# One wide matmul for two of three partial products in the last stage, results folded afterwards, one operand sum on POOL

## The chip, the cores and the metric

The kernel runs on one core of a Trainium2 chip. The metric is the time of one execution on the device in microseconds, the median of several runs. TensorE (PE in the rows, PEld for its weight loads) multiplies, VectorE (DVE in the rows) and ScalarE (ACT) work on tiles in SBUF and PSUM, GpSimd (POOL) on tiles in SBUF, and SyncE (SP) issues most of the DMA transfers.

## The reference

Attention over chunks of 32 positions, then two feed-forward blocks on 3072 tokens of 512 features, all in float32:

```python
x = attention(q, k, v, mem_k, mem_v)          # 3072 x 512
h = x @ w_in;  x = (h * tanh(softplus(h))) @ w_out
xn = x / sqrt(mean(x * x) + 1e-6) * rms_g
g = xn @ w_gate;  val = xn @ w_val            # 512 x 1536 each
out = (silu(g) * val) @ w_out                 # 1536 x 512
```

The change lies in the last product, `(silu(g) * val) @ w_out`.

## The kernel before

Every large product is done with two devices. First, a float32 operand is split into a high part (a rounded copy, made by ScalarE) and a low part (the rest, a subtraction on VectorE), and a product is the sum of high by high, high by low and low by high. Secondly, the matrices are cut into 2 x 2 blocks and multiplied in Strassen-Winograd fashion: seven block products instead of eight, on operands that are sums of blocks, and the results are put together by additions.

The last stage works in 12 units, one for each of three pairs of token groups and four row ranges (`units`, L1215, and the loop at L1252). A unit makes 256 rows of the output. Its input h was written to DRAM by the stage before and is loaded as four blocks of 128 x 768 (`h_load`, L867): a unit with an even number into the buffers raw, raw, sm and s, one with an odd number into parts of one weight slot, w. From the blocks come seven operands, which this text calls T1 to T7 by the number of the product (`h_pieces`, L885, and `sum_one`, L586). T1, T2, T3 and T7 are split from a block or a first sum, T5, T6 and T4 from a chain of three differences that are written into the same block: a difference on VectorE (L888), the high part on ScalarE (L153), the low part on VectorE (L154), then the next difference. The operands of unit n + 1 are made while TensorE works on unit n, one piece after each product (`preparing`, L1217). There are eight T buffers.

A product (`mul` in `group3`, L906) runs over six blocks of 128 features with three matmuls each, at L912 to L914: the high part of T with the high and the low part of the weights, and the low part of T with the high part of the weights. T is the operand that is loaded, the weights stream, and all three add into the same 256 columns of a PSUM bank. The weights w lie in SBUF as (7, 2, 256) per feature block: seven block operands, each with its high and its low part side by side. The results are put together in `group`, L643: two copies to SBUF on ScalarE (L649, L657), additions that read PSUM on VectorE (L654, L665, L668, L670), one sum on POOL (L669), and a last copy on ScalarE (L921). Two stores per unit are issued two pieces later (`store_later`, L104).

A scheduler of the framework orders the instructions of every engine by a timeline of its own (L19); each engine then executes its queue in that order. It issues the seven products of a unit in the order 1, 5, 6, 2, 4, 7, 3 and the operands as T1, T5, T6, T2, T4, T7, T3.

Of the kernel before, what the change touches and what calls it, by code (L numbers as in the profile page):

```python
# [13 lines left out]
ALU = mybir.AluOpType  # L14
# [10 lines left out]
W_AT = {1: 0, 2: 1, 4: 2, 3: 3, 5: 4, 6: 5, 7: 6}  # L25
# [4 lines left out]
def tile_kernel(  # L30
# [15 lines left out]
    nc = tc.nc  # L46
# [57 lines left out]
    def store_later(dst, src):  # L104
        late.append((tick[0] + 2, dst, src))
# [12 lines left out]
    wtab, wslot = {}, {}  # L118
# [37 lines left out]
    jobs, raws, n_load, n_raw, start = [], [], [0], [10 ** 6], [True]  # L156
# [387 lines left out]
    def att_list(j):  # L544

        out = []
        t0 = TPP * j
        for s in range(TPP + 4):
            for op, lag in (("e", 4), ("d", 3), ("c", 2), ("b", 1), ("a", 0)):
                t = t0 + s - lag  # L550
                if t0 <= t < t0 + TPP:
                    if op == "a" and t % SPB == 0:
                        out.append([(att_a0, t)])
                    out.append([(att_ops[op], t), (att_ops[op + "1"], t)])
        return out
# [13 lines left out]
    def s_new():  # L569
        return late_pools["s"].tile([128, 2, N2], F32, tag="s", name="s")  # L570

    def v_new(i):
        return late_pools[("gr", "gl")[i % 2]].tile([128, 2, N2], F32, tag="v", name="v")

    def c_new():
        return late_pools["c"].tile([128, N2], F32, tag="c", name="c")
# [9 lines left out]
    def sum_one(j, p, src, new, dram, tab):  # L586
        cols = src.shape[2]
        size = src.shape[1] * cols
        t = new()
        if isinstance(t, tuple):  # L590
            split(src, *t)
            for l in range(2):
                store_later(dram[:, p - 1, l].bitcast(F32), t[l].bitcast(F32))
            return
        v = t.rearrange("p l a n -> p l (a n)")[:, :, 0:size]
        v = v.rearrange("p l (a n) -> p l a n", n=cols)
        split(src, v[:, 0], v[:, 1])
        if dram is not None:
            store_later(dram[:, p - 1].bitcast(F32), t.bitcast(F32))
        tab[j, p] = v  # L600
# [42 lines left out]
    def group(mul, banks, n_, c12, c21, c22, temps, five_first=False):  # L643

        X, Y, Z, V = banks
        x, y, z, vv = (b_[:, 0:n_] for b_ in banks)
        s1, u2, z5 = temps()
        mul(1, X, True)
        nc.scalar.copy(s1, x)  # L649
        yield  # L650
        for p in (5, 6) if five_first else (6, 5):
            if p == 6:
                mul(6, Y, True)
                nc.vector.tensor_tensor(u2, y, s1, op=ALU.add)  # L654
            else:
                mul(5, Z, True)
                nc.scalar.copy(z5, z)  # L657
            yield
        mul(4, V, True)
        yield  # L660
        mul(2, X, False)
        yield
        mul(7, Y, False)
        u3 = s1
        nc.vector.tensor_tensor(u3, y, s1, op=ALU.add)  # L665
        yield
        mul(3, Z, False)
        nc.vector.tensor_tensor(c12, z, u2, op=ALU.add)  # L668
        nc.gpsimd.tensor_tensor(c22, u3, z5, op=ALU.add)  # L669
        nc.vector.scalar_tensor_tensor(  # L670
            c21, vv, -1.0, u3, op0=ALU.mult, op1=ALU.add
        )
        yield
# [25 lines left out]
    def run(parts, between):  # L699
        while parts:  # L700
            for part in list(parts):
                if next(part, "end") == "end":
                    parts.remove(part)
                else:
                    between()
# [3 lines left out]
    def group_banks(of):  # L709
        g = n_group[0]  # L710
        n_group[0] += 1
        return [bk[(4 * g + of - 4 + i) % of] for i in range(4)]
# [21 lines left out]
    n_v = [0]  # L734
# [23 lines left out]
    class Feed:  # L758
# [34 lines left out]
        def next(self, s):  # L793
            self.load(s + 3)
            self.split(s + 3)
            self.load(s + 5)
            return self.out.pop(0)
# [87 lines left out]
    def h_pieces(n):  # L885
        b11, b21, b12, b22 = hraw.pop(n)
        one = lambda p, src: sum_one(n, p, src, t_new2, None, ttab_h)
        sub = lambda out, a, b: nc.vector.tensor_tensor(out, a, b, op=ALU.subtract)  # L888
        early = [lambda: one(1, b11), lambda: sub(b11, b12, b11), lambda: sub(b12, b22, b12)]

        def p5():
            one(5, b11)
            sub(b11, b22, b11)

        def p6():
            one(6, b11)
            sub(b11, b11, b21)

        return early, [p5, p6, lambda: one(2, b21), lambda: one(4, b11),
                       lambda: one(7, b12), lambda: one(3, b22)]  # L900

    def group3(n, j, r, between):
        o = s_new()
        o = [o[:, a, :] for a in range(2)]

        def mul(p, bank_, first):  # L906
            t = ttab_h[n, p]
            ps = bank_[:, 0:256]
            more = dict(skip_group_check=not first)
            for f in range(HG):  # L910
                w = wtab["o2", f][:, W_AT[p]]
                nc.tensor.matmul(ps, t[:, 0, f], w[:, 0], start=first and f == 0, stop=False, **more)  # L912
                nc.tensor.matmul(ps, t[:, 0, f], w[:, 1], start=False, stop=False, **more)  # L913
                nc.tensor.matmul(ps, t[:, 1, f], w[:, 0], start=False, stop=f == HG - 1, **more)  # L914

        banks = group_banks(8)
        c11 = banks[0][:, 0:256]
        c12, c21, c22 = o[1][:, 0:256], o[0][:, 256:512], o[1][:, 256:512]
        run([group(mul, banks, 256, c12, c21, c22, lambda: (c_new()[:, 0:256], c12, c22),
                   True)], between)  # L920
        nc.scalar.copy(o[0][:, 0:256], c11)  # L921
        for a in range(2):
            row = (2 * j + a) * N2 + 128 * r
            store_later(out[row:row + 128, :], o[a])
# [24 lines left out]
    HG = F2 // 2  # L949
# [12 lines left out]
    first = att_list(0)  # L962
# [82 lines left out]
    units = [(1, i) for i in range(NHEAD)]  # L1045
    units += [(b, i) for i in (3, 4, 7, 5, 6) for b in range(2)]
    at = {u: 4 * n + 4 for n, u in enumerate(units)}
    more = {}
# [6 lines left out]
    more = {}  # L1055
# [10 lines left out]
    more = {}  # L1066
# [60 lines left out]
    for s, (m, i) in enumerate(steps):  # L1127
        t = feed.next(s)
# [18 lines left out]
        if m == NB2 - 1 and i in (1, 3, 5, 6):  # L1147
            row_slots.clear()
            f, u = {1: (2, 5), 3: (3, 6), 5: (4, 3), 6: (5, 2)}[i]
# [65 lines left out]
    units = [(j, r) for j in jback for r in range(NSUB2)]  # L1215

    def preparing(n, between):  # L1217

        st = dict(n=0)

        def fn():
            between()
            st["n"] += 1
            if st["n"] == 1:
                st["early"], st["rest"] = h_pieces(n)
                for call in st["early"]:
                    call()
            elif st["rest"]:
                st["rest"].pop(0)()

        return fn
# [20 lines left out]
    for n, (j, r) in enumerate(units):  # L1252
        if 0 < n < len(units) - 1:
            h_load(n + 1, *units[n + 1])
        group3(n, j, r, preparing(n + 1, flush) if n + 1 < len(units) else flush)
# [32 lines left out]
```

## Time and profile before

| | us |
|---|---|
| median of three runs (1165.23 to 1170.05) | 1168.31 |
| span of the profiled execution | 1167.0 |
| TensorE busy over the span | 1142.3 (98%) |
| VectorE busy | 824.7 (71%) |
| ScalarE busy | 628.7 (54%) |
| POOL busy | 183.3 (16%) |
| first matmul of the last stage | 979.76 |
| start of the last addition on VectorE | 1162.77 |

The page gives the span, which is 1.3 us under the median of the runs. Shares over the span are means over stages with different limits. The last stage takes the last 187 us of the span, so the windows and timelines of that stage are what counts. A matmul's row lasts longer than the distance to the next one, because matmuls are pipelined; the distance of starts is what it costs.

### The profile page before, as it was taken

The numbers are of one execution on the slowest core, as the hardware profiler recorded it, in microseconds if no ns is written. First come the engines' busy times: TensorE is split into PE (matmuls) and PEld (weight loads), VectorE is DVE, ScalarE is ACT, GpSimd is POOL, SyncE is SP. The second block draws the span as 40 slices with busy tenths as digits, with TensorE's granted clock in tenths as the row PEclk, the third lists the DMA queues.
The fourth block names the chain that finished last, engine by engine and source line by source line (L and its number), as shares of the span: only waits on it lengthen the run. The fifth ranks groups of instructions, "written<-read, shape, count | busy, mean of one in ns | idle before, by whom it ended". The sixth has DMA issues, their size and how long they took to land.

```text
span 1167.0 us, 22953 instructions
## 1 busy us (share of the span) xinstructions
PE 1142.3 (98%) x9052; PEld 1007.0 (86%) x9052; DVE 824.7 (71%) x1254; ACT 628.7 (54%) x1008; POOL 183.3 (16%) x165
## 2 busy tenths in 40 slices
PE   6899999999999999999999999999999999999998
PEld 4789999999999888888878778888888888999998
DVE  3555798844746876766786765967896857888883
ACT  4566666543555887667775543544454433444441
POOL 3011222310132321010011121110211111000000
PEclk9799999999999999999999999999999999999999
DMA  9889699899488764594599398999899879655421
GB/s 197 171 228 224 183 303 258 230 307 290 151 300 295 257 217 161 172 378 152 199 362 408 126 345 325 349 410 355 316 361 371 316 276 332 191 148 146 145 90 37
DMA packets 213276, 294.20 MB, mean 252 GB/s; under 512 B 104240, under 2 KB 160560, under 8 KB 204336
## 3 DMA queue, kind: packets, MB, share of 16 engines
q1 hardware_dynamic: 210864, 284.34, 73.6%
q0 software_dynamic: 2304, 8.39, 2.3%
q8 instruction: 71, 1.16, 0.4%
q14 instruction: 37, 0.30, 0.1%
HBM read 181.80 MB, written 110.89 MB: 251 GB/s over the span
## 4 chain that ended last, share of the span: by engine, by line
PE 83%; DVE 7%; DMA 5%; ACT 3%; issue 2%; SPq 0%; POOL 0%; ACTq 0%; DVEq 0%
PE bk L639 14%; PE bk L640 13%; PE bk L641 13%; PE bk L914 4%; PE bk L913 4%; PE bk L912 4%; PE bk L755 4%; PE bk L756 4%; PE bk L754 4%; PE bkp L639 2%; PE bkp L641 2%; PE bkp L640 2%; PE bkp L506 1%; PE bkp L457 1%; PE bkp L755 1%
## 5 line engine op out<-in xcount | busy, mean ns | idle before, releaser
L639 PE MATMUL bk<-T,w 128*128 128x384 f32 (+1 forms) x860 | 315.2, 370 | 0.7 <-ACT c L657 0.7
L640 PE MATMUL bk<-T,w 128*128 128x384 f32 (+1 forms) x860 | 311.3, 362 | 0.0
L641 PE MATMUL bk<-T,w 128*128 128x384 f32 (+1 forms) x860 | 308.3, 362 | 0.0
L639 PEld LDWEIGHTS bk<-T,w 128*128 128x128 f32 x860 | 162.3, 189 | 19.9 <-ACT c L657 1.0
L640 PEld LDWEIGHTS bk<-T,w 128*128 128x128 f32 x860 | 162.2, 189 | 16.5 <-DVE T L154 0.3
L641 PEld LDWEIGHTS bk<-T,w 128*128 128x128 f32 x860 | 161.8, 188 | 15.7
L913 PE MATMUL bk<-w,T 128*128 128x256 f32 x396 | 111.9, 283 | 0.0
L914 PE MATMUL bk<-w,T 128*128 128x256 f32 x396 | 111.9, 283 | 0.0
L912 PE MATMUL bk<-w,T 128*128 128x256 f32 x396 | 111.9, 283 | 0.0
L755 PE MATMUL bk<-T,w 128*128 128x512 f32 x276 | 107.5, 390 | 0.2 <-DVE T L154 0.2
L756 PE MATMUL bk<-T,w 128*128 128x512 f32 x276 | 107.1, 389 | 0.0
L754 PE MATMUL bk<-T,w 128*128 128x512 f32 x276 | 105.8, 389 | 0.0
L669 POOL TENSOR_TENSOR v<-c,v 128x512 f32<-128x512 f32 x36 | 54.7, 1519 | 289.2 <-DVE c L665 238.8
L665 DVE TENSOR_TENSOR c<-bk,c 128x512 f32<-128x512 f32 (+2 forms) x72 | 43.0, 597 | 51.2 <-PE bk L641 38.6
L912 PEld LDWEIGHTS bk<-w,T 128*128 128x128 f32 x396 | 76.0, 192 | 0.1
L913 PEld LDWEIGHTS bk<-w,T 128*128 128x128 f32 x396 | 76.0, 192 | 0.1
L914 PEld LDWEIGHTS bk<-w,T 128*128 128x128 f32 x396 | 76.0, 192 | 0.0
L649 ACT COPY c<-bk 128x512 f32<-128x512 f32 (+2 forms) x72 | 37.1, 516 | 69.6 <-POOL v L669 24.7
L154 DVE TENSOR_TENSOR T<-s,T 128x1024 fp32r<-128x1024 f32 (+1 forms) x50 | 63.1, 1269 | 14.3 <-ACT T L153 14.2
L782 ACT ACTIVATE s<-s 128x1024 f32<-128x1024 f32 x44 | 46.4, 1060 | 29.7 <-DMA s<-g_scratch 29.5
L755 PEld LDWEIGHTS bk<-T,w 128*128 128x128 f32 x276 | 51.8, 188 | 11.3 <-DVE T L154 0.6
L754 PEld LDWEIGHTS bk<-T,w 128*128 128x128 f32 x276 | 51.8, 188 | 10.8
(228 smaller groups left out, 2287.1 us busy)
## 6 DMA issues: line engine op xcount, KB each, us to landing
T<-nt_scratch SPq DMA_DIRECT2D x35, 1024.0 KB
g_scratch<-g SPq DMA_DIRECT2D x64, 384.0 KB
s<-g_scratch SPq DMA_DIRECT2D x46, 512.0 KB
h_scratch<-s SPq DMA_DIRECT2D x36, 512.0 KB
w<-wg SPq DMA_DIRECT2D x10, 1792.0 KB
wg<-w SPq DMA_DIRECT2D x30, 512.0 KB
raw<-in_moe_w_out_dram SPq DMA_DIRECT2D x28, 512.0 KB
nt_scratch<-T SPq DMA_DIRECT2D x14, 1024.0 KB
```

The costliest lines, as they stand in the source:

```text
L154: keep((eng or nc.vector).tensor_tensor(lo, src, hi.bitcast(F32), op=ALU.subtract))
L639: nc.tensor.matmul(ps, whi, xh, start=first and kk == 0, stop=False, **more)
L640: nc.tensor.matmul(ps, whi, xl, start=False, stop=False, **more)
L641: nc.tensor.matmul(ps, wlo, xh, start=False, stop=kk == 1, **more)
L669: nc.gpsimd.tensor_tensor(c22, u3, z5, op=ALU.add)
L754: nc.tensor.matmul(ps, ahi, bhi, start=start, stop=False)
L755: nc.tensor.matmul(ps, ahi, blo, start=False, stop=False)
L756: nc.tensor.matmul(ps, alo, bhi, start=False, stop=stop)
L782: nc.scalar.activation(x, g, self.act)
L912: nc.tensor.matmul(ps, t[:, 0, f], w[:, 0], start=first and f == 0, stop=False, **more)
L913: nc.tensor.matmul(ps, t[:, 0, f], w[:, 1], start=False, stop=False, **more)
L914: nc.tensor.matmul(ps, t[:, 1, f], w[:, 0], start=False, stop=f == HG - 1, **more)
```

## The change

In `group3` one matmul takes the high part of T with both halves of the weights, 512 columns, so that high by high lies in columns 0 to 255 of a bank and high by low in 256 to 511. A second matmul of 256 columns adds low by high to the upper half. All results stay 512 columns wide through the additions, and at the end a fold adds the upper to the lower half: four folds per unit on POOL (in the last unit on VectorE). The copy of product 5 goes to a tile of the pool `v`, the output's first block is copied at 512 columns to a tile of the pool `c`. In `h_pieces` the second difference of the early ones, b22 - b12, is made on POOL.

```diff
--- before.py
+++ after.py
@@ -885,8 +885,8 @@
     def h_pieces(n):
         b11, b21, b12, b22 = hraw.pop(n)
         one = lambda p, src: sum_one(n, p, src, t_new2, None, ttab_h)
-        sub = lambda out, a, b: nc.vector.tensor_tensor(out, a, b, op=ALU.subtract)
-        early = [lambda: one(1, b11), lambda: sub(b11, b12, b11), lambda: sub(b12, b22, b12)]
+        sub = lambda out, a, b, eng=nc.vector: eng.tensor_tensor(out, a, b, op=ALU.subtract)
+        early = [lambda: one(1, b11), lambda: sub(b11, b12, b11), lambda: sub(b12, b22, b12, nc.gpsimd)]
 
         def p5():
             one(5, b11)
@@ -902,23 +902,54 @@
     def group3(n, j, r, between):
         o = s_new()
         o = [o[:, a, :] for a in range(2)]
+        n_v[0] += 1
+        z5 = v_new(n_v[0])[:, 0, :]
+        end = n == len(units) - 1
 
         def mul(p, bank_, first):
             t = ttab_h[n, p]
-            ps = bank_[:, 0:256]
-            more = dict(skip_group_check=not first)
             for f in range(HG):
-                w = wtab["o2", f][:, W_AT[p]]
-                nc.tensor.matmul(ps, t[:, 0, f], w[:, 0], start=first and f == 0, stop=False, **more)
-                nc.tensor.matmul(ps, t[:, 0, f], w[:, 1], start=False, stop=False, **more)
-                nc.tensor.matmul(ps, t[:, 1, f], w[:, 0], start=False, stop=f == HG - 1, **more)
-
-        banks = group_banks(8)
-        c11 = banks[0][:, 0:256]
-        c12, c21, c22 = o[1][:, 0:256], o[0][:, 256:512], o[1][:, 256:512]
-        run([group(mul, banks, 256, c12, c21, c22, lambda: (c_new()[:, 0:256], c12, c22),
-                   True)], between)
-        nc.scalar.copy(o[0][:, 0:256], c11)
+                w = wtab["o2", f][:, W_AT[p]].rearrange("p l f -> p (l f)")
+                nc.tensor.matmul(bank_, t[:, 0, f], w, start=first and f == 0, stop=False,
+                                 skip_group_check=True)
+                nc.tensor.matmul(bank_[:, 256:512], t[:, 1, f], w[:, 0:256], start=False,
+                                 stop=f == HG - 1, skip_group_check=True)
+
+        def fold(out, x):
+            (nc.vector if end else nc.gpsimd).tensor_tensor(out, x[:, 0:256], x[:, 256:512], op=ALU.add)
+
+        def parts():
+            x, y, z, vv = group_banks(8)
+            s1 = c_new()
+            mul(1, x, True)
+            nc.scalar.copy(s1, x)
+            yield
+            mul(5, z, True)
+            nc.scalar.copy(z5, z)
+            yield
+            mul(6, y, True)
+            nc.vector.tensor_tensor(o[1], y, s1, op=ALU.add)
+            yield
+            mul(4, vv, True)
+            yield
+            mul(2, x, False)
+            c11 = c_new()
+            nc.scalar.copy(c11, x)
+            yield
+            mul(7, y, False)
+            nc.vector.tensor_tensor(s1, y, s1, op=ALU.add)
+            nc.vector.scalar_tensor_tensor(o[0], vv, -1.0, s1, op0=ALU.mult, op1=ALU.add)
+            nc.gpsimd.tensor_tensor(z5, s1, z5, op=ALU.add)
+            fold(o[0][:, 256:512], o[0])
+            fold(o[0][:, 0:256], c11)
+            yield
+            mul(3, z, False)
+            nc.vector.tensor_tensor(o[1], z, o[1], op=ALU.add)
+            fold(o[1][:, 0:256], o[1])
+            fold(o[1][:, 256:512], z5)
+            yield
+
+        run([parts()], between)
         for a in range(2):
             row = (2 * j + a) * N2 + 128 * r
             store_later(out[row:row + 128, :], o[a])
```

VectorE's queue while it makes the operands of an even unit (raw, sm, s), before; bk and bkp are PSUM banks, T an operand with its low part:

```order
L154 TENSOR_TENSOR T<-raw,T 128x768
L888 TENSOR_TENSOR raw<-sm,raw 128x768
L888 TENSOR_TENSOR sm<-s,sm 128x768
L654 TENSOR_TENSOR s<-bk_83,c 128x256
L154 TENSOR_TENSOR T<-raw,T 128x768
L888 TENSOR_TENSOR raw<-s,raw 128x768
L154 TENSOR_TENSOR T<-raw,T 128x768 x2
L888 TENSOR_TENSOR raw<-raw 128x768
L665 TENSOR_TENSOR c<-bk_83,c 128x256
L670 SCALAR_TENSOR_TENSOR s<-bk_85,c 128x256
L154 TENSOR_TENSOR T<-raw,T 128x768
L668 TENSOR_TENSOR s<-bk_84,s 128x256
```

The same stretch of VectorE's queue after:

```order
L154 TENSOR_TENSOR T<-raw,T 128x768
L888 TENSOR_TENSOR raw<-sm,raw 128x768
L154 TENSOR_TENSOR T<-raw,T 128x768
L888 TENSOR_TENSOR raw<-s,raw 128x768
L940 TENSOR_TENSOR c<-bk_83,c 128x512
L941 SCALAR_TENSOR_TENSOR s<-bk_85,c 128x512
L947 TENSOR_TENSOR s<-bk_84,s 128x512
L154 TENSOR_TENSOR T<-raw,T 128x768 x2
L888 TENSOR_TENSOR raw<-raw 128x768
L154 TENSOR_TENSOR T<-raw,T 128x768
L931 TENSOR_TENSOR s<-bk_87,c 128x512
L154 TENSOR_TENSOR T<-sm,T 128x768
```

The difference `sm<-s,sm` is gone from the queue, and the additions from PSUM (L931, L940, L941, L947) have 512 columns and stand elsewhere: L931 between the low parts of T4 and T7, where L654 stood in front of T5.

POOL's queue in the last stage, before (its end):

```order
L823 TENSOR_TENSOR w<-w 128x512
L824 TENSOR_TENSOR w<-w 128x512
L825 TENSOR_TENSOR w<-w 128x512
L669 TENSOR_TENSOR v<-c,v 128x512 x36
L669 TENSOR_TENSOR s<-c,s 128x256 x12
```

POOL's queue after, for an even and an odd unit from the middle of the stage (lines from L919 on are those of the kernel after):

```order
L888 TENSOR_TENSOR sm<-s,sm 128x768
L942 TENSOR_TENSOR v<-c,v 128x512
L919 TENSOR_TENSOR s<-s 128x256 x2
L919 TENSOR_TENSOR s<-c 128x256
L919 TENSOR_TENSOR s<-v 128x256
L888 TENSOR_TENSOR w<-w 128x768
L942 TENSOR_TENSOR v<-c,v 128x512
L919 TENSOR_TENSOR s<-s 128x256
L919 TENSOR_TENSOR s<-c 128x256
L919 TENSOR_TENSOR s<-s 128x256
L919 TENSOR_TENSOR s<-v 128x256
```

One instruction per unit became six: the difference (L888), the sum of product 5 (L942) and four folds (L919), the odd unit's in another order than the even one's.

## Rows read from the trace of the kernel before

**Rows 1.** VectorE and the others by window, the last stage

```profile
core 0: us, PE busy (x) PEld busy (x) DVE busy (x) ACT busy (x) POOL busy (x), PEclk, DMA share, GB/s
985.00:1160.00 175.00, 175.00 (x1461) 175.00 (x1460) 131.65 (x167) 72.49 (x112) 10.54 (x12) 1.00 0.46 136
```

**Rows 2.** Timeline of TensorE: start us, us, engine, line, tiles, shape, count

```profile
975.00 0.39 PE L641 MATMUL bkp<-T,w 128*128 128x512 f32 x1
...
976.36 0.39 PE L641 MATMUL bk<-T,w 128*128 128x512 f32 x1
...
979.54 0.39 PE L641 MATMUL bk<-T,w 128*128 128x512 f32 x1
979.76 0.28 PE L912 MATMUL bk<-w,T 128*128 128x256 f32 x1
...
1149.73 0.28 PE L913 MATMUL bk<-w,T 128*128 128x256 f32 x1
...
1151.89 0.28 PE L913 MATMUL bk<-w,T 128*128 128x256 f32 x1
```

**Rows 3.** Timeline of VectorE, operands of units 1 to 5, same columns

```profile
992.70 0.96 DVE L154 TENSOR_TENSOR T<-w,T 128x768 fp32r<-128x768 f32 x1 [4.40 <-ACT T L153]
...
1005.77 0.95 DVE L154 TENSOR_TENSOR T<-raw,T 128x768 fp32r<-128x768 f32 x1
1006.76 0.96 DVE L888 TENSOR_TENSOR raw<-sm,raw 128x768 f32<-128x768 f32 x1
1007.75 0.96 DVE L888 TENSOR_TENSOR sm<-s,sm 128x768 f32<-128x768 f32 x1
1008.67 0.96 DVE L154 TENSOR_TENSOR T<-raw,T 128x768 fp32r<-128x768 f32 x1
...
1018.28 0.95 DVE L154 TENSOR_TENSOR T<-w,T 128x768 fp32r<-128x768 f32 x1
...
1031.80 0.95 DVE L154 TENSOR_TENSOR T<-raw,T 128x768 fp32r<-128x768 f32 x1
...
1050.54 0.96 DVE L888 TENSOR_TENSOR w<-w 128x768 f32<-128x768 f32 x1
1052.45 1.83 DVE L154 TENSOR_TENSOR T<-w,T 128x768 fp32r<-128x768 f32 x2 [0.95 <-ACT T L153]
```

**Rows 4.** Waits, 980 to 1165 us: who waited for whom, us in total, times, longest

```profile
ACT T L153 <- DMA w<-h_scratch: 5.8, 1, 5.8
```

**Rows 5.** Instructions of line 912 by shape

```profile
L912 PE MATMUL bk<-w,T x396: 277/283/283, 979.8 to 1162.2; 128*128 128x256 f32 x198
...
L912 PE MATMUL bkp<-w,T x108: 283/283/283, 983.3 to 1147.1; 128*128 128x256 f32 x108
```

**Rows 6.** Timeline of VectorE, additions from PSUM, 512 and 256 columns

```profile
976.79 0.69 DVE L665 TENSOR_TENSOR c<-bk,c 128x512 f32<-128x512 f32 x1
977.40 0.68 DVE L654 TENSOR_TENSOR s<-bk,c 128x512 f32<-128x512 f32 x1
...
1041.58 0.42 DVE L670 SCALAR_TENSOR_TENSOR s<-bk,c 128x256 f32<-128x256 f32 x1
1041.91 0.41 DVE L668 TENSOR_TENSOR s<-bk,s 128x256 f32<-128x256 f32 x1
```

**Rows 7.** Instructions of line 669 on POOL: ns min/median/max, first and last start

```profile
L669 POOL TENSOR_TENSOR v<-c,v x36: 1286/1317/3272, 650.8 to 984.0; 128x512 f32<-128x512 f32 x36
...
L669 POOL TENSOR_TENSOR s<-c,s x12: 737/740/1336, 998.0 to 1161.2; 128x256 f32<-128x256 f32 x12
```

**Rows 8.** Timeline of VectorE beside a POOL sum

```profile
940.64 2.38 DVE L154 TENSOR_TENSOR w<-sm,w 128x512 fp32r<-128x512 f32 x2
...
1025.00 2.36 DVE L154 TENSOR_TENSOR T<-w,T 128x768 fp32r<-128x768 f32 x2
```

**Rows 9.** Timeline of POOL at the same places

```profile
940.02 1.84 POOL L669 TENSOR_TENSOR v<-c,v 128x512 f32<-128x512 f32 x1 [11.37 <-DVE c L665]
...
1025.30 1.24 POOL L669 TENSOR_TENSOR s<-c,s 128x256 f32<-128x256 f32 x1 [13.47 <-DVE c L665]
```

**Rows 10.** Timeline of VectorE, its last instruction

```profile
1162.77 0.42 DVE L668 TENSOR_TENSOR s<-bk,s 128x256 f32<-128x256 f32 x1 [1.22 <-PE bk L914]
```

## The prediction

> **What bounds the kernel now.** I read the busy shares by window first. Between 985 and 1160 us, the last stage, TensorE is busy all the time at full granted clock, VectorE 131.65 of 175 us, ScalarE 72 and POOL 10.5 [rows 1]. So TensorE sets the pace, and the next engine is VectorE. The timeline of TensorE gives the price of a matmul: 18 of 256 columns start in 2.16 us (1149.73 to 1151.89), 0.120 us each, and six of 512 columns in 1.36 us, 0.2267 us each, and the row of 256 columns behind one of 512 starts 0.22 us after it [rows 2]. Twice the columns costs 0.107 us more, which leaves 0.0133 us that every matmul pays whatever its width.
>
> The second question is how far VectorE is ahead, since it makes the operands T. The first one of unit 1 starts at 992.70, of units 2, 3 and 4 at 1005.77, 1018.28 and 1031.80 [rows 3]: 13.03 us per unit, while TensorE needs 42 x 0.360 = 15.12. VectorE gains 2.1 us on TensorE in each unit; that is all the room there is. It begins with almost none: unit 1's first cast waited 5.8 us for the h blocks to arrive [rows 4].
>
> **TensorE.** A product on one block of w was 3 x 0.120 = 0.360 us and is 0.2267 + 0.120 = 0.3467. There are 12 x 7 x 6 = 504 of them (396 + 108 rows of L912 [rows 5]): 504 x 0.0133 = 6.7 us less, and a unit is 42 x 0.3467 = 14.56 us. Whether the 13.3 ns belong to the matmul or to its change of weights makes no difference: one of each goes per product. The Trainium skill, "TensorE: Matmul & The Clock Gate", section "Back-to-back issue gap", gives a warm spacing of columns / 2.4 GHz plus about 2.5 ns; by it the saving would be an estimated 504 x 0.0025 = 1.3 us. The rows show 13.3 ns, and I go by them.
>
> **VectorE's own work.** Results are now 512 columns wide. In a row of such instructions each takes 0.61 us where one of 256 takes 0.33 (976.79 to 977.40, 1041.58 to 1041.91 [rows 6]). Four of 0.60 replace three of 0.33: +1.4 us per unit. The sum that goes to POOL gives back nothing: from the first difference to the low part of T5 it is 1.91 us with that sum in between (1006.76 to 1008.67) and 1.91 where none is in between (1050.54 to 1052.45) [rows 3], because ScalarE's cast lies there. ScalarE's wider copies fit into its idle half.
>
> I walk the queue of an even unit as the order after has it: independent instructions of 768 columns follow in 0.88 us (1.83 for two), dependent ones in 0.99, the difference to its low part is 1.91 [rows 3]. T1 0.00, first difference 0.99, T5 2.90, second difference 3.89, L940 4.76, L941 5.47, L947 6.07, T6 6.67, T2 7.54, third difference 8.41, T4 10.32, L931 11.19, T7 11.79, T3 12.66, next unit 13.53. The odd unit's order comes to 13.14. The same walk over the order of before gives 12.4 and 12.8, with 0.5 for its one POOL sum about 13.1, against 13.03 measured. So without POOL the units would be made in 13.3 us, under 14.56.
>
> **POOL.** This is the term that decides. Before, POOL does one sum of 256 columns per unit; after, one of 768, one of 512 and four of 256. Alone it takes 0.74 us for 256 and 1.29 to 1.32 for 512 [rows 7], so about 1.87 for 768 (estimate along that line), 6.1 us per unit. Where a POOL sum meets a VectorE instruction that reads two SBUF tiles, one stands still. At 1025.00 two low parts take 2.36 us instead of 1.83 while the sum of 256 beside them takes 1.24 instead of 0.74; at 940.64 two of 512 take 2.38 instead of 0.61 + 0.68, beside a sum of 512 with 1.84 [rows 3, 6, 8 and 9]. POOL waits for the running instruction, goes next, and VectorE then loses 0.53 us to 256 columns, 1.09 to 512, and by the same step 1.65 to 768: 4.9 us per unit if all of it lands on such instructions. Low parts and differences are of that kind; the four additions from PSUM are not, and while VectorE waits for a cast nothing is lost either.
>
> The walk again, with POOL in its order. The 768 sum can start when the first difference has ended (1.95, plus 0.2 until POOL moves) and holds to 3.8: T5 goes from 2.90 to 3.81. Second difference 4.80, L940 5.67, L941 6.38, L947 6.98. The sum of 512 runs from 6.5 to 7.6 under these three, so T6 loses 0.05 and starts at 7.63. The first two foldings are queued behind it; each gets in behind a VectorE instruction: T2 9.13, third difference 10.63 (0.63 late each, with POOL's start). The third folding fits into the wait for T4's cast, the fourth half: T4 12.86, L931 13.73, T7 14.33, T3 15.20, next unit 16.07. That is 2.5 us of the 4.9. In the odd unit L941 stands behind the second difference, and the last folding meets T7: 0.91 + 0.15 + 0.63 + 0.63 + 0.37 + 0.63 = 3.3, next unit 16.46. Mean 16.27 us, 1.7 over TensorE's 14.56. The bounds of this term are 0 (13.3 us) and 4.9 (18.2); I take 2.9, since the walk reproduces before.
>
> The Trainium skill, "SBUF — State Buffer", section "Who interferes with whom", has it that the loser blocks for the whole instruction of the other. By its full durations a fold would cost 0.74 instead of 0.53, an estimated 1 us more per unit than my walk. Rows 8 and 9 bear out the standstill, at the smaller price.
>
> **Sum.** VectorE now paces the stage. Unit 1's first operand still starts at 992.70, since it waits for a transfer that the change doesn't touch. Ten cycles later, at 992.7 + 162.7 = 1155.4, unit 11 starts; T4 is complete 13.6 later, at 1169.0, and TensorE, which takes the products in the order 1, 5, 6, 2, 4, 7, 3, has three left: 3 x 2.08 = 6.2. The last addition starts at 1175.3 where it was 1162.77 [rows 10]: +12.5. Behind it was one instruction of 0.42; now 0.71 for the wide addition to be done and two folds, 0.34 + 0.42: +1.05 to the output's transfers. Together +13.5 on the span of 1167.0; the page gives the span alone, and the runs' median is 1.3 over it. So 1168.3 + 13.5 = 1182.
>
> **Rivals.**
> *Operands keep ahead.* If the POOL sums fall into VectorE's waits for casts (2.0 us per unit) and under its four PSUM additions (2.4), all but 0.5 us is covered, a cycle is 13.8, TensorE stays the bound, and the time is 1168.3 - 6.7 + 1.05 = 1162.7. For it: of the walk's six meetings in an even unit, one costs nothing and one 0.05. Against it: foldings are issued back to back, and what is behind them are low parts. It decides the other way only if a cycle stays under 14.7. 20%, split evenly by the bound of half a per cent.
> *Half covered.* The end of the stage moves by 10.8 us per us of cycle (ten cycles and five sixths of one), so a cycle of 15.0 gives the time of before and 15.5 gives 1174. If foldings run later than I have them, into the next unit's first wait, 0.8 to 1.2 us of my 2.9 go: 1168 to 1174. 13%.
> *POOL in a heap.* If nothing is covered, 18.2 us per cycle, the time is about 1203. For it, POOL's own queue: late foldings delay the 768 sum, and T7 needs that. Against it, POOL has 10 us between the two. 5%.
> *The wide matmul brings nothing* (pitch 0.240): 1169 if TensorE were the bound. Rows 2 show 512 columns at 0.2267 in this kernel; 2%.
>
> **How the numbers follow.** The main case has 60%, with its own range of 1174 to 1191 (cycles of 15.5 to 17.1). Half a per cent, 5.8 us, is what a measurement here can tell from no change. Faster than 1162.5: half of the first rival, 0.10. Within: the other half, the half-covered case and the wide matmul's, 0.25. Slower: 0.65. The range goes from 1163 to 1191; it leaves out most of the first rival and the heap.
>
> **What would show it.** Right: in the last stage TensorE idles for some 1.5 us per unit, before the first matmul that needs a low part, released by VectorE; first low parts of units two apart are 32 to 33 us apart; low parts of 768 columns have a mean of 1.2 us or more instead of 1.0; POOL is busy for over 6 us per unit. TensorE's matmuls themselves start 0.227 and 0.120 apart. Wrong: TensorE busy without a gap and units at 14.6 us (the first rival), POOL's sums long but low parts at 0.95 (VectorE goes first, and POOL pays), or a first operand of unit 1 that comes well before 992, which would give VectorE a lead to live on.

## Result and the profile after

The changed kernel takes 1181.61 us (median of six runs, 1176.43 to 1185.49), the kernel before 1168.36 beside it (six runs, 1165.23 to 1170.05): a ratio of 1.0105, 95% interval 1.0088 to 1.0123. It is slower, at nearly the predicted time. The profiled execution took 1182.14 us with a span of 1180.4, 13.4 us over the span of before.

First the busy time by window in the last stage, in the columns of [rows 1]:

```profile
985.00:1175.00 190.00, 180.00 (x994) 151.28 (x992) 161.41 (x162) 78.58 (x114) 93.62 (x68) 1.00 0.44 129
```

TensorE, which had no gap before, is idle for some 10 us, at full granted clock. VectorE has gone from 75% to 85%, POOL from 10.54 us to 93.62. The waits of that stretch (engine, tile and line; what ended the wait; us in total, times, longest) say who is late:

```profile
PEld bk L915 <- DVE T L154: 11.0, 13, 1.7
PE bk L915 <- DVE T L154: 6.8, 13, 1.4
...
PEld bkp L915 <- DVE T L154: 4.2, 5, 1.0
PE bkp L915 <- DVE T L154: 2.6, 5, 0.7
```

These are TensorE's waits for a low part, 9.4 us on its matmuls (6.8 + 2.6). Between them the matmuls run at their pace, as TensorE's timeline shows behind the last wait:

```profile
1166.01 0.40 PE L913 MATMUL bk<-w,T 128*128 128x512 f32 x1
1166.25 0.28 PE L915 MATMUL bk<-w,T 128*128 128x256 f32 x1
...
1168.13 0.40 PE L913 MATMUL bk<-w,T 128*128 128x512 f32 x1
```

Six pairs in 2.12 us are 0.353 each; over all pairs without a stall the mean is 0.3494. Between 1075.70 and 1091.42 VectorE's queue makes an even unit, the walk of the prediction in real rows (start us, us, engine, line, operation, tiles, [idle before <- what ended it]):

```profile
1075.70 0.95 DVE L154 TENSOR_TENSOR T<-raw,T 128x768 fp32r<-128x768 f32 x1
1076.68 0.96 DVE L888 TENSOR_TENSOR raw<-sm,raw 128x768 f32<-128x768 f32 x1
1078.59 1.78 DVE L154 TENSOR_TENSOR T<-raw,T 128x768 fp32r<-128x768 f32 x1 [0.95 <-ACT T L153]
1080.41 0.96 DVE L888 TENSOR_TENSOR raw<-s,raw 128x768 f32<-128x768 f32 x1
1081.28 0.68 DVE L940 TENSOR_TENSOR c<-bk,c 128x512 f32<-128x512 f32 x1
1082.00 0.69 DVE L941 SCALAR_TENSOR_TENSOR s<-bk,c 128x512 f32<-128x512 f32 x1
1082.61 0.68 DVE L947 TENSOR_TENSOR s<-bk,s 128x512 f32<-128x512 f32 x1
1083.21 2.43 DVE L154 TENSOR_TENSOR T<-raw,T 128x768 fp32r<-128x768 f32 x2
1085.56 1.49 DVE L888 TENSOR_TENSOR raw<-raw 128x768 f32<-128x768 f32 x1
1088.01 1.16 DVE L154 TENSOR_TENSOR T<-raw,T 128x768 fp32r<-128x768 f32 x1 [0.96 <-ACT T L153]
1089.09 0.68 DVE L931 TENSOR_TENSOR s<-bk,c 128x512 f32<-128x512 f32 x1
...
1091.42 0.94 DVE L154 TENSOR_TENSOR T<-w,T 128x768 fp32r<-128x768 f32 x1
```

And POOL's in the same stretch, with its 768 sum (L888), its sum of 512 (L942) and the four folds (L919):

```profile
1077.72 1.84 POOL L888 TENSOR_TENSOR sm<-s,sm 128x768 f32<-128x768 f32 x1 [4.22 <-DVE raw L888]
1082.11 1.30 POOL L942 TENSOR_TENSOR v<-c,v 128x512 f32<-128x512 f32 x1 [2.55 <-DVE c L940]
1083.37 2.86 POOL L919 TENSOR_TENSOR s<-s 128x256 f32<-128x256 f32 x2
1086.19 1.45 POOL L919 TENSOR_TENSOR s<-c 128x256 f32<-128x256 f32 x1
1087.61 0.74 POOL L919 TENSOR_TENSOR s<-v 128x256 f32<-128x256 f32 x1
```

Lay one over the other. The low part of T5 is ready at 1078.59, but POOL holds on until 1079.56 and the 0.95 us become 1.78. The sum of 512 runs under additions from PSUM, and neither loses anything. The first three folds lie beside the low parts of T6 and T2 and the third difference: 2.43 instead of 1.83 and 1.49 instead of 0.95, while POOL needs 1.43 a fold instead of 0.74. The last fold lies mostly in a wait for a cast; T4's low part loses 0.21. That is 2.2 us in this unit. The odd one before it (from 1059.70) loses 2.9 by the same reading, 0.89 of it in the low part of T5 and the rest to the folds:

```profile
1062.55 1.84 DVE L154 TENSOR_TENSOR T<-w,T 128x768 fp32r<-128x768 f32 x1 [0.91 <-ACT T L153]
...
1066.82 2.42 DVE L154 TENSOR_TENSOR T<-w,T 128x768 fp32r<-128x768 f32 x2 [0.36 <-ACT T L153]
1069.16 1.49 DVE L888 TENSOR_TENSOR w<-w 128x768 f32<-128x768 f32 x1
...
1071.61 2.70 DVE L154 TENSOR_TENSOR T<-w,T 128x768 fp32r<-128x768 f32 x2 [0.36 <-ACT T L153]
```

### The profile page after: what moved, and what is told of

Read it like the earlier page. It is cut to its first block, busy times and chain, and to the rows that moved or that the text cites. A ratio compares the mean times of both kernels' runs of the same rounds, so it can differ in the third digit from the quotient of the medians.

```text
span 1180.4 us, 22026 instructions
## 1 busy us (share of the span) xinstructions
PE 1143.6 (97%) x8548; PEld 979.7 (83%) x8548; DVE 853.1 (72%) x1246; ACT 633.8 (54%) x1008; POOL 265.3 (22%) x221
## 4 chain that ended last, share of the span: by engine, by line
PE 66%; DVE 16%; DMA 7%; ACT 5%; issue 4%; SPq 1%; POOL 0%; ACTq 0%; DVEq 0%; POOLq 0%
PE bk L639 13%; PE bk L640 13%; PE bk L641 13%; DVE T L154 6%; PE bk L755 4%; PE bk L756 4%; PE bk L754 4%; ACT T L153 2%; DMA s<-g_scratch 2%; PE bkp L639 2%; PE bkp L640 2%; PE bkp L641 2%; DVE w L888 1%; PE bkp L506 1%; PE bkp L755 1%
## 5 line engine op out<-in xcount | busy, mean ns | idle before, releaser
L913 PE MATMUL bk<-w,T 128*128 128x512 f32 x396 | 138.8, 395 | 0.0
L915 PE MATMUL bk<-w,T 128*128 128x256 f32 x396 | 109.6, 284 | 6.8 <-DVE T L154 6.8
L913 PEld LDWEIGHTS bk<-w,T 128*128 128x128 f32 x396 | 73.5, 188 | 15.6
L915 PEld LDWEIGHTS bk<-w,T 128*128 128x128 f32 x396 | 74.6, 188 | 12.5 <-DVE T L154 11.0
L154 DVE TENSOR_TENSOR T<-s,T 128x1024 fp32r<-128x1024 f32 (+1 forms) x50 | 62.5, 1258 | 14.2 <-ACT T L153 14.2
L665 DVE TENSOR_TENSOR c<-bk,c 128x512 f32<-128x512 f32 (+1 forms) x60 | 38.0, 633 | 43.8 <-PE bk L641 41.6
L154 DVE TENSOR_TENSOR T<-w,T 128x768 fp32r<-128x768 f32 x42 | 53.5, 1295 | 15.2 <-ACT T L153 15.2
L153 ACT CAST T<-w 128x768 fp32r<-128x768 f32 x42 | 33.3, 832 | 55.5 <-DVE w L888 49.3
L649 ACT COPY c<-bk 128x512 f32<-128x512 f32 (+1 forms) x60 | 32.5, 543 | 56.4 <-POOL v L669 24.5
```

The costliest lines, as they stand in the source:

```text
L153: keep(nc.scalar.copy(hi, src))
L154: keep((eng or nc.vector).tensor_tensor(lo, src, hi.bitcast(F32), op=ALU.subtract))
L913: nc.tensor.matmul(bank_, t[:, 0, f], w, start=first and f == 0, stop=False, skip_group_check=True)
L915: nc.tensor.matmul(bank_[:, 256:512], t[:, 1, f], w[:, 0:256], start=False, stop=f == HG - 1, skip_group_check=True)
```

## The experiments

All times are medians, each with its ratio to runs of the kernel before on the same chip (1167.84 beside sum_back to no_folds, 1167.97 beside folds_write to narrow_last); the ratio is estimated from all runs and differs a little from the quotient of the two medians. "Stage" runs from the first to the last start of a matmul of the last stage; "cycle" is the distance of the first low parts (T1) of units 3 and 11 divided by eight; "low part" is the mean duration of L154 between 995 and 1155 us.

| kernel | median us | ratio [95%] | stage us | cycle us | low part ns |
|---|---|---|---|---|---|
| before | 1168.36 | 1 | 182.7 | 13.03 (units 1 to 4) | 996 |
| after | 1181.61 | 1.0105 [1.0088, 1.0123] | 193.5 | 15.86 | 1243 |
| sum_back | 1170.55 | 1.0021 [1.0003, 1.0039] | 183.0 | 15.01 | 1123 |
| folds_vector | 1169.78 | 1.0011 [0.9992, 1.0029] | 181.0 | 14.87 | 1023 |
| both_vector | 1164.11 | 0.9971 [0.9949, 0.9992] | 178.3 | 14.72 | 964 |
| no_folds | 1163.63 | 0.9969 [0.9946, 0.9992] | 179.3 | 14.49 | 977 |
| folds_write | 1164.12 | 0.9962 [0.9945, 0.9979] | 178.7 | 14.49 | 977 |
| folds_twice | 1179.79 | 1.0098 [1.0076, 1.0121] | 194.8 | 16.24 | 1237 |
| sum_only | 1167.88 | 0.9996 [0.9983, 1.0009] | 183.2 | 13.58 (units 1 to 4) | 1118 |
| narrow_last | 1165.35 | 0.9970 [0.9957, 0.9983] | 179.1 | 14.71 | 964 |

The theory, called the port theory in the expectations: VectorE's instructions on two SBUF tiles and POOL's sums exclude each other, and that is what makes the units longer. Two rivals: VectorE is late by its own work (wider additions, its order), and TensorE itself is the bound.

### sum_back: the 768 sum back on VectorE

```diff
-        early = [..., lambda: sub(b12, b22, b12, nc.gpsimd)]
+        early = [..., lambda: sub(b12, b22, b12)]
```

> The kernel after with b22 - b12 back on VectorE; folds stay on POOL. Port theory (a POOL sum stops VectorE's instructions that read two SBUF tiles): the sum of 768 no longer meets T5's low part (0.91 us per unit) and costs VectorE nothing itself, since it fills the wait for the cast: operand cycle 16.0 to about 15.1 us, time about 1172. Rival, VectorE's own queue (its wider additions and the order set the pace, POOL does not matter): 0.9 us per unit more on VectorE, about 1191. Rival, TensorE (the wide matmuls are slow): no change, 1182.

Measured: 1170.55, with a cycle of 15.01 instead of 15.86. VectorE has one more instruction of 768 columns in every unit and finishes each unit 0.85 us sooner. Low parts (L154, tiles of w) between 995 and 1155, by line and shape, after and then here (count | busy us, mean ns | idle before them, and its cause):

```profile
L154 DVE TENSOR_TENSOR T<-w,T 128x768 fp32r<-128x768 f32 x36 | 45.6, 1287 | 13.5 <-ACT T L153 13.5
```

```profile
L154 DVE TENSOR_TENSOR T<-w,T 128x768 fp32r<-128x768 f32 x39 | 44.5, 1162 | 8.4 <-ACT T L153 8.4
```

The mean falls by 125 ns. The rest of VectorE's queue has the same order in both kernels. Its own work cannot be what makes VectorE late.

### folds_vector and both_vector: the folds on VectorE

```diff
-            (nc.vector if end else nc.gpsimd).tensor_tensor(out, x[:, 0:256], x[:, 256:512], op=ALU.add)
+            nc.vector.tensor_tensor(out, x[:, 0:256], x[:, 256:512], op=ALU.add)
```

folds_vector keeps the 768 sum on POOL, both_vector has it on VectorE too.

> The kernel after with all folds on VectorE; the 768 sum stays on POOL. Port theory: four folds cost 1.9 us per unit as standstills (mean of the walk's 2.3 and 1.6) and 4 x 0.33 = 1.3 as VectorE's own work: cycle 16.0 to about 15.4, time about 1175. VectorE's own queue: 1.3 more, cycle 17.3, about 1196. TensorE: no change, 1182.

> The sum and the folds on VectorE; POOL keeps only the 512 sum of product 5. Port theory: 16.0 - 0.9 - 1.9 + 1.3 = 14.5, at TensorE's own pace: 1164 to 1169. VectorE's own queue: 16.0 + 0.9 + 1.3 = 18.2, about 1205. TensorE: 1182.

Measured: 1169.78 and 1164.11. The first came out better than expected: in its order L940, an addition from PSUM, lies in the first wait for a cast, beside the sum on POOL, and loses nothing to it; the low part of T5 behind it loses 0.37 us (1.32 instead of 0.95 at 1068.71) where it lost 0.83. The second, with the sum and the folds on VectorE, beats both kernels, by 0.3% over before. Its low parts, and its window from 995 to 1155:

```profile
L154 DVE TENSOR_TENSOR T<-w,T 128x768 fp32r<-128x768 f32 x40 | 37.9, 970 | 0.8 <-ACT T L153 0.8
```

```profile
995.00:1155.00 160.00, 159.74 (x911) 138.52 (x909) 150.34 (x205) 74.47 (x106) 19.55 (x12) 1.00 0.44 126
```

The same window of after:

```profile
995.00:1155.00 160.00, 150.79 (x831) 126.58 (x830) 141.09 (x141) 69.76 (x101) 82.50 (x60) 1.00 0.45 130
```

VectorE is busier (150.34 us against 141.09) and yet TensorE has next to no gap. Its timeline shows the four folds in 1.43 us (1068.18 to 1069.61), and that VectorE now waits for TensorE:

```profile
1068.18 0.75 DVE L919 TENSOR_TENSOR s<-s 128x256 f32<-128x256 f32 x2
1068.85 0.42 DVE L919 TENSOR_TENSOR s<-c 128x256 f32<-128x256 f32 x1
1069.19 0.42 DVE L919 TENSOR_TENSOR s<-v 128x256 f32<-128x256 f32 x1
...
1072.96 0.69 DVE L931 TENSOR_TENSOR s<-bk,c 128x512 f32<-128x512 f32 x1 [0.47 <-PE bk L915]
```

In after, the even unit shown above loses 1.35 us to the same folds on POOL (0.60 + 0.54 + 0.21), and the odd one 2.0 (0.59 + 0.54 + 0.87): VectorE saves nothing by giving them away, and on the mean of the two loses some 0.25 us.

### no_folds and folds_write: no folds, and POOL work that only writes

Both start from sum_back. no_folds leaves the four folds out; folds_write puts two fills in the place of each:

```diff
-            (nc.vector if end else nc.gpsimd).tensor_tensor(out, x[:, 0:256], x[:, 256:512], op=ALU.add)
+            for _ in range(2):
+                nc.gpsimd.memset(out, 0.0)
```

> Leaves the four folds of each unit out (the upper halves of the results are not added), sum on VectorE. Port theory: cycle 16.0 - 0.9 - 1.9 = 13.2, so TensorE is never short of operands and shows its own price: 0.347 us per pair of matmuls would give about 1162, the 0.351 to 0.353 that stretches of the trace after show about 1164. VectorE's own queue: 16.9, about 1191. TensorE: 1182.

> sum_back with each fold replaced by two POOL fills of the fold's output (256 columns each, so the upper halves are not added; POOL writes SBUF and reads none). Port theory (what collides is the reading of a second tile): VectorE runs as without folds, low parts of 768 columns at 0.99 us or less on average against 1.12 in sum_back, cycle under TensorE's 14.7, time like no_folds, about 1163. Rival (any POOL work on SBUF, or POOL's queue being full, slows VectorE): as sum_back, cycle 15.0, 1171.

Measured: 1163.63 and 1164.12, both with a cycle of 14.49, not 13.2: TensorE sets the pace. The 14.49 includes units in which the operands still gain on TensorE; from unit 5 to unit 11 it is 14.65, TensorE's 42 x 0.3494 = 14.67. In folds_write POOL fills (L920) while low parts run. Its timeline of POOL and VectorE, then its lines from 995 to 1155:

```profile
1071.15 2.08 POOL L920 MEMSET s<- 128x256 f32 x8
1071.16 1.82 DVE L154 TENSOR_TENSOR T<-raw,T 128x768 fp32r<-128x768 f32 x2
1072.89 0.95 DVE L888 TENSOR_TENSOR raw<-raw 128x768 f32<-128x768 f32 x1
```

```profile
L154 DVE TENSOR_TENSOR T<-w,T 128x768 fp32r<-128x768 f32 x41 | 38.9, 973 | 6.6 <-ACT T L153 6.6
...
L920 POOL MEMSET s<- 128x256 f32 x88 | 23.3, 310 | 19.9 <-DVE s L948 19.9
```

Two low parts in 1.82 and a difference in 0.95, the undisturbed times, with POOL at work until 1073.23. So it is not POOL's activity or its place in the program that stops VectorE. What a fold has and a fill has not is reads from SBUF; a fold alone also takes longer (0.74 us against 0.31), which these runs don't separate. The Trainium skill, "SBUF — State Buffer", section "Who interferes with whom", says that a VectorE instruction with two SBUF inputs contends with a POOL instruction that reads SBUF, and not with one that only writes; these rows agree.

### folds_twice: each fold on POOL twice

From sum_back; in two of the four folds a half is thereby added twice.

```diff
-            (nc.vector if end else nc.gpsimd).tensor_tensor(out, x[:, 0:256], x[:, 256:512], op=ALU.add)
+            for _ in range(1 if end else 2):
+                (nc.vector if end else nc.gpsimd).tensor_tensor(out, x[:, 0:256], x[:, 256:512], op=ALU.add)
```

> sum_back with every POOL fold executed twice, apart from the last unit's. Port theory: four more folds per unit at 0.53 to 0.63 us each, less what falls into waits for casts: cycle 15.0 to between 16.5 and 17.2, time about 1186 to 1194. Rival (VectorE's own queue sets the pace): no change, 1171.

Measured: 1179.79, in the right direction but under the expected range: +1.23 us per unit, 0.31 for an extra fold. The price of a meeting is unchanged (2.44 and 1.49 as in after), but not every extra fold makes a meeting of its own. POOL and VectorE in an odd unit:

```profile
1064.34 2.44 DVE L154 TENSOR_TENSOR T<-w,T 128x768 fp32r<-128x768 f32 x2 [0.35 <-ACT T L153]
1064.51 2.87 POOL L920 TENSOR_TENSOR s<-s 128x256 f32<-128x256 f32 x2
1066.70 1.49 DVE L888 TENSOR_TENSOR w<-w 128x768 f32<-128x768 f32 x1
1067.45 2.16 POOL L920 TENSOR_TENSOR s<-c 128x256 f32<-128x256 f32 x2
1068.12 0.68 DVE L948 TENSOR_TENSOR s<-bkp,s 128x512 f32<-128x512 f32 x1
1069.16 2.69 DVE L154 TENSOR_TENSOR T<-w,T 128x768 fp32r<-128x768 f32 x2 [0.36 <-ACT T L153]
```

The two folds from 1067.45 to 1069.61 lie for about half of their time under an addition from PSUM (0.68, undisturbed) and in a wait for a cast. The expectation had counted nearly every extra fold as a full meeting.

VectorE's queue has the same order in after, sum_back and folds_twice, but for the sum, so these three can be added up against each other. Over units 3 to 10 the low parts and differences take, beyond 0.95 us each, 2.54 us per unit in after, 1.70 in sum_back and 2.93 in folds_twice. The steps between them, -0.84 and +1.23, are those of the cycle (-0.85 and +1.23). In folds_write it is 0.06.

### sum_only: the kernel before with the 768 sum on POOL

```diff
-        early = [..., lambda: sub(b12, b22, b12)]
+        early = [..., lambda: sub(b12, b22, b12, nc.gpsimd)]
```

(`sub` takes the engine as in the change.)

> The kernel before with b22 - b12 on POOL and nothing else. As predicted (the sum costs VectorE nothing where it stood, and on POOL it holds up T5's low part by some 0.9 us): operands are made at 13.5 to 14 us per unit while VectorE catches up, instead of 13.03, TensorE (15.12 us per unit) stays the bound, time as before, 1168. Rival (the move relieves VectorE by a difference): 12.1 us per unit, the time as before too; the operand cycle of units 1 to 4 tells them apart.

Measured: 1167.88, the same as before. Its operands of units 1 to 4 are 13.58 us apart instead of 13.03 [rows 3], and the low part of T5 stands still beside the sum:

```profile
1006.54 0.96 DVE L888 TENSOR_TENSOR raw<-sm,raw 128x768 f32<-128x768 f32 x1
1007.58 1.85 POOL L888 TENSOR_TENSOR sm<-s,sm 128x768 f32<-128x768 f32 x1 [9.09 <-DVE raw L888]
1008.46 1.79 DVE L154 TENSOR_TENSOR T<-raw,T 128x768 fp32r<-128x768 f32 x1 [0.96 <-ACT T L153]
```

The same stall that is on the path in after costs nothing here, since TensorE needs 15.12 us a unit and the operands are ahead.

### narrow_last: both_vector with the last unit as before

```diff
-        run([parts()], between)
+        if end:
+            ...
+            run([group(mul1, banks, 256, c12, c21, c22, lambda: (c_new()[:, 0:256], c12, c22),
+                       True)], between)
+            nc.scalar.copy(o[0][:, 0:256], banks[0][:, 0:256])
+        else:
+            run([parts()], between)
```

(`mul1` is the old `mul`.)

> both_vector with the last unit in the form of before (narrow matmuls, no folds): from the last matmul's start to the end of the span 4.8 us instead of 6.3, while the last unit's matmuls take 42 x 0.0105 = 0.44 longer: about 1 us less than both_vector, 1163. If the folds behind the last matmul cost nothing, as both_vector, 1164.

Measured: 1165.35, 0.9970 of before; both_vector's 0.9971 has an interval that covers it. In the profile the tail is shorter: from the last matmul's start to the end of the span 4.1 us (1156.92 to 1161.0), where both_vector has 6.0 (1154.46 to 1160.5), while the stage is longer (179.1 instead of 178.3). The medians show nothing of the difference. Inconclusive.

## Why the prediction was right

*The pace.* Right: VectorE sets it, through POOL. The walk gave 16.27 us per unit; over units 1 to 11 it is 16.02 (994.71 to 1154.86), over units 3 to 11 15.86. The meetings cost 2.2 and 2.9 us where the walk had 2.5 and 3.3. They lie at the places it named, but that in the odd unit the sum of 512 cost nothing (the walk's second term there, 0.15); the rest of the difference is in the folds, each a little cheaper than the walk's (0.54 to 0.60 instead of 0.63, T4's 0.21 instead of 0.32, the odd unit's last pair 0.87 instead of 1.00). By the full block that the prediction cites, and that the Trainium skill states in that section for VectorE's two-port modes, a fold would have cost 0.74; the rows show less. The signs came out near what was named: TensorE's waits of 9.4 us are 0.9 per unit and not 1.5, first low parts of units two apart are 31.7 us apart (32 to 33 predicted), the low parts' mean is 1243 ns, and POOL is busy for some 8 us per unit. Both rivals to the port fall: VectorE's own work by sum_back and both_vector, TensorE by both_vector, where it runs without gaps at 14.72.

*The two parts.* With the other part on VectorE, the sum on POOL costs 5.7 us (folds_vector against both_vector) and the folds 6.4 (sum_back against both_vector); together they cost 17.5 (after against both_vector). The same sum beside folds on POOL costs 11.1 (after against sum_back). Each of these differences is uncertain by some 3 us, as the intervals of the ratios show; the stages of the profiles give 2.7, 4.7, 15.2 and 10.5 in their place. Either way the two parts together cost more than their sum. The cycles say why: the first part lifts VectorE's cycle just over TensorE's pace (14.72 to 14.87 or 15.01) and is partly taken up by the room below it; the second is paid in full (15.86).

*TensorE.* Right in kind, too large: a pair is 0.3494 us and not 0.3467, so 504 x (0.360 - 0.3494) = 5.3 us are to be had and not 6.7. In both_vector most of that arrives: its stage is 4.4 us shorter than that of before, its time 0.29%, 3.4 us. The saving of 10.6 ns per pair lies nearer to the 13.3 of the rows than to the 2.5 of the formula that the prediction cites. Why the pairs vary between 340 and 361 ns is open.

*VectorE's own work.* One sentence was wrong: before also has four additions from PSUM, so the wider results cost 4 x 0.27 = 1.1 us per unit, not 1.4. The walk had all four in it, and nothing hangs on the sentence. That the sum on POOL gives VectorE nothing, because ScalarE's cast lies there, is shown by sum_only and by T5's row in after.

*The start and the end.* That the forecast came within half a microsecond is luck: three errors cancel. Unit 1's first operand came at 994.71, not 992.70. The stage's first matmul is also 1.1 us later, and over the profiles here it came anywhere from 976.1 to 982.6, so this much may be a difference between executions; of the other 0.9, 0.5 is a longer wait of the first cast for the h blocks (6.3 us instead of 5.8), and the rest is not explained. The ten cycles were 10 x 0.25 = 2.5 us shorter. And a fold on VectorE, treated below, held up the last addition by some 0.5. So the last addition started at 1175.17, predicted 1175.3 [rows 10]:

```profile
1173.58 0.69 DVE L941 SCALAR_TENSOR_TENSOR s<-bk,c 128x512 f32<-128x512 f32 x1
1174.30 0.95 DVE L919 TENSOR_TENSOR s<-s 128x256 f32<-128x256 f32 x1
1175.17 0.68 DVE L947 TENSOR_TENSOR s<-bk,s 128x512 f32<-128x512 f32 x1
...
1176.62 0.42 DVE L919 TENSOR_TENSOR s<-v 128x256 f32<-128x256 f32 x1
```

From there to the end of the span it is 5.2 us where it was 4.2: +1.0, predicted 1.05. But a fold of the last unit stands ahead of that addition and takes 0.95 instead of 0.42, since POOL's sum of 512 (1173.69, 1.28 us) lies beside it; the addition starts 0.83 us behind the last matmul's start, where before it was 0.31. The prediction did not have this.

*The range.* The rivals with a shorter cycle did not come about, and sum_back shows how near they were: at a cycle of 15.01 the time is 1170.55, 2.7 us over its before, where the half-covered case put the time of before at 15.0.

## What to carry to other kernels

Work moved from VectorE to POOL is not taken off VectorE when both read SBUF: each POOL sum stops a two-tile instruction for most of its own, longer time, so four folds cost VectorE 1.35 or 2.0 us from POOL, by the order of the unit, and 1.43 us on VectorE itself. Price a moved instruction by what lies beside it: under additions from PSUM, in a wait for a cast, or as a fill that reads nothing it costs nothing. And find the room first: the same sum on POOL costs nothing in the kernel before, some 3 to 6 us beside the wide matmul with the folds on VectorE, and some 11 with the folds on POOL.

## What the runs showed of the hardware

- A POOL sum of 256 columns beside a chain of low parts takes 1.43 us instead of 0.74 and costs VectorE 0.54 to 0.6; a sum of 768 keeps its 1.84 when it comes first, and a low part that comes 0.97 us before its end loses 0.83.
- POOL fills (306 to 318 ns each for 256 columns) beside two-tile instructions of VectorE cost neither engine anything that the rows show (973 ns on the mean for a low part).
- A matmul of 512 columns and one of 256 in turn start 0.3494 us apart per pair on the mean, where rows of one width gave 0.2267 + 0.120 = 0.3467.
